# Another order of all steps, other conversion paths and more products of constants in an RWKV-7 and GELU kernel

## The chip, the cores and the metric

The kernel runs on one core of a Trainium2 chip. The metric is the device time of one execution in microseconds, the median of several runs. A core has five engines with a queue of instructions each: PE (matrix products, with a weight load PEld ahead of each), DVE (vector work), ACT (scalar functions and copies), POOL (general work), and SP, which here only issues DMA transfers. An engine takes its queue in order, and waits on semaphores where an instruction needs another engine's result.

## What is computed

Two blocks follow each other. The first is a recurrence over 768 time steps for 4 batches and 8 heads, with a 40 by 40 state for each; the second is a feed-forward block on the 3072 rows that come out.

```python
for t in range(S):
    y[:, :, t] = np.einsum('bhd,bhde->bhe', rt, state)
    Sa = np.einsum('bhde,bhe->bhd', state, at)
    state_decay = state * wt[:, :, None, :] - np.einsum('bhd,bhe->bhde', Sa, bt)
    state = state_decay + np.einsum('bhd,bhe->bhde', vt, kt)
...
h = x @ w_in                                   # (3072, 320) @ (320, 2048)
g = 0.5 * h * (1.0 + erf(h * inv_sqrt2))
return (g @ w_out).astype(np.float32)          # (3072, 2048) @ (2048, 320)
```

r, k, v, w, a and b are 32-bit floats. `w_in` and `w_out` come as 64-bit floats, 5.24 MB each, and the kernel makes 32-bit floats of them on the chip.

## The kernel before

Time is cut into 12 chunks of 64 steps. For each chunk all 32 batch-head pairs are worked on together. The products of the recurrence inside a chunk become small matrix products, and the dependence inside a chunk becomes the inverse of a triangular matrix per pair. The state passes from chunk to chunk. The output of each chunk, 256 rows, goes through the feed-forward block as soon as it is there.

**Order.** Every step is a small function, registered by its name, that issues the instructions of one piece of work. `order` (line 17) returns one long list of names with numbers, such as `nm.3` or `mh.0.2`, and the last two lines of the kernel perform them in that order. The scheduler is set to manual for all five engines, so each engine's queue is this list, restricted to the engine's own steps. The list also sets the use of four PSUM buffers (`bank0` to `bank3`): a step that calls `take` gets the buffer that has been given back longest, and waits for its last reader.

**Steps of a chunk c.**

- Loads, all on SP: `Lw La Lb Lk Lr LV` (line 433 and following, 320 KB each). From chunk 3 or 4 on some tensors are also loaded in a second layout (`Lwt Lbt Lkt Lv`).
- Decays: `lg` (log on ACT, L665), `cu` and `wT` (running sums of the logs as products with a mask, PE), `ec` and `ew` (exponentials, ACT, L722 and L708), `sb` and `sk` (scaled b and k, DVE or POOL).
- Transposes: `ta tb tk tr tv` on PE and `tm` on PE (L731); the copies out of PSUM are `sa sn kc rc vc tn`. From chunk 3 or 4 on most transposes run on DVE (L737).
- Products of pairs: `nm am vm` on PE, with masks applied by `nk ak vk` on DVE (L845).
- Inverse: for chunk 0 by squaring on PE, five rounds `qm.0` to `qm.4` with `qc qz qb qa` between them on ACT and DVE. For the others on POOL: `Ns` and `Nl` bring the blocks through DRAM into `Nb`, `ic` (L907 and L909) eliminates 31 columns with two instructions each, `Is`, `If` and `Ij` bring the result back into `Tt` and `T2`, and `tc_` on DVE, `jm`, `km` on PE and `jc kt0 kt1` join the blocks.
- State: `av` and `xm` (PE), `xc0 xc1` (copies), `sm` (PE), `sc` (DVE, L1108), `pk` and `pb` (PE), then `oa od om` (DVE) and `oc tm tn ym yc` make the next state and the output. `ox` moves parts of the output across partitions by DMA into `xt`.
- Feed-forward: `mh.c.p` for p from 0 to 7, 20 products each (L1231), reads `xt` and half of `w_in`'s converted form; `ge` is GELU (L1236). For chunks 0 to 2 the second product is `pm.c.n` (L1347, 16 products of 320 columns, four per chunk). From chunk 3 on it is seven products `m1` to `m7` of eight 160-column pieces each (L1270), with sums `s1` to `s4`, `e1` to `e6`. `so` writes the result.

**Conversion.** `w_in` is converted in units 0 to 9 of 512 columns, `w_out` in units 10 to 25 of 320 columns. They come by `Lf`, `Lf5` (units 0 to 9) and `Ls.f` (unit f + 10). For each unit `cp cm cs` (DVE) and `ce` (ACT) take the exponent, the mantissa and the sign. The mantissa's low part is then added and the result scaled by one of three paths:

- `cv`: two DVE instructions (L617, L618).
- `cl`, `cn` (ACT, L625, L632) and `cg`: two POOL instructions (L640, L641).
- `cl`, `cn` (ACT), `cx`: two PE products with the identity, and `cy`: one DVE product. No unit takes this path in the kernel before.

**Products of constants.** `warm_first` (six instructions) and `warm.4.i` (two instructions each) multiply constants into a PSUM buffer that nobody reads. There are 9 of the second kind before the change. The masks and constants themselves are set by POOL and DVE at the start (`identity`, `sums_mask`, `pads_...`, `warm_set`).

Of the kernel before, what the change touches and what calls it, by code (L numbers as in the profile page):

```python
# [16 lines left out]
def order(chunks, first_seven):  # L17
    return """
        of_half_set Lw.0 pads_a.0 sums_mask lg.0 cu.0 ec.0 Lb.0 sb.0 warm_set pads_w.0 pads_extra.2 pads_extra.0
        pads_extra.1 identity upper_mask pads_rows.0 pads_r.0 pads_VR.1 pads_r.1 first_ones.0 Tt_zero bias_set  # L20
# [4 lines left out]
        Lf.2.0.1 Lf.2.1.1 Lf5.1.1 Lk.1 warm.4.11 qa.1 qz.1 qb.1.0.v ce.0 cn.3 ce.3 ec.1 qb.1.1.a cs.0 cs.3 sb.1
        qm.2 qa.2 qz.2 qb.2.0.v warm.4.3 ta.1 warm.4.19 tb.1 iz.1 cg.3 sk.0.p sa.1 cp.5 cv.0 cm.5 cl.5 qc.2
        qb.2.1.a qm.3 qz.3 qb.3.0.v qa.3 tk.0 ce.5 sn.1 nm.1 kc.0 qb.3.1.a cn.5 nk.1 cs.5 cp.2 tr.0 cg.5 qm.4
        rc.0 ce.2 cl.4 qc.3 cl.7 tv.0 qa.4 cs.2 cp.7 cm.2 ce.7 cm.7 cn.7 ql cs.7 am.0 jm.0 ak.0 cv.2 cp.4 cm.4
# [1357 lines left out]
```

## Time and profile before

| | |
|---|---|
| median of 3 runs | 672.73 us (672.18 to 674.0) |
| the profiled execution | 673.18 us |
| its span, first to last instruction | 671.5 us |
| mean granted TensorE clock | 0.982 |
| POOL busy | 382.7 us (57%) |
| queue 1, all loads and stores | 73.78 MB, 60.2% of 16 DMA engines' span |

A profile page gives for each engine the time that it was busy, the span in 40 equal slices (a digit is the busy share in tenths), the clock that PE was granted, the share of the DMA engines, and groups of instructions by line. An L and a number name a line of the kernel. The timeline lists instructions by start and duration in us, with the number of them after an x, and in brackets how long the engine was idle before and what released it ("issue" where nothing that the profile shows did). Matmuls overlap, so a duration of a group reaches to the end of its last one.

### The profile page before, as it was taken

How to read it: one execution, taken by the hardware profiler on the slowest of the kernel's cores; microseconds unless marked ns; L12 is line 12 of the kernel's file. 1: busy time of each engine (PE TensorE's matmuls, PEld its weight loads, DVE VectorE, ACT ScalarE, POOL GpSimd, SP SyncE). 2: the span in 40 equal slices, each digit the busy share in tenths (PEclk: the TensorE clock that was granted, in tenths of full speed). 3: DMA queues.
4: the chain of work that ended last, by engine and by line, in shares of the span. 5: the costliest groups of instructions: out<-in, count | busy, mean ns of one | idle time of the engine just before them, and what ended most of it. 6: DMA issues, size and time to landing. Idle time of an engine off the chain costs nothing.

```text
span 671.5 us, 28177 instructions
## 1 busy us (share of the span) xinstructions
PE 643.9 (96%) x12480; PEld 560.8 (84%) x12480; DVE 421.5 (63%) x528; ACT 262.9 (39%) x329; POOL 382.7 (57%) x803
## 2 busy tenths in 40 slices
PE   4797889999999999999999999999999999999997
PEld 3576778888778878898898998997998988988987
DVE  1699988671664755885884777773885863723403
ACT  4456636522352452552623545242252344033040
POOL 4245873780585873871886860884872877830000
PEclk9796979999999999999999999999999999999999
DMA  9989488848867758647949757748658564130100
GB/s 153 159 169 163 98 189 170 152 91 137 151 112 138 137 109 148 138 86 136 155 85 163 141 115 136 124 86 155 130 108 141 109 121 84 38 60 3 26 16 21
DMA packets 302934, 78.10 MB, mean 116 GB/s; under 512 B 282556, under 2 KB 297692, under 8 KB 302812
## 3 DMA queue, kind: packets, MB, share of 16 engines
q1 hardware_dynamic: 301748, 73.78, 60.2%
q0 software_dynamic: 864, 2.36, 2.1%
q8 instruction: 98, 1.61, 1.0%
q14 instruction: 24, 0.20, 0.1%
q10 hardware_dynamic: 200, 0.16, 0.1%
HBM read 62.62 MB, written 9.70 MB: 108 GB/s over the span
## 4 chain that ended last, share of the span: by engine, by line
PE 80%; DVE 4%; SPq 2%; DMA 2%; issue 2%; POOL 1%; ACT 1%; DVEq 0%; POOLq 0%; ACTq 0%
PE bank L1231 28%; PE bank L196 22%; PE bank L1270 21%; PE bank L1347 8%; PE bank L731 2%; DMA v_pairs<-in_w_dram 1%; SPq L446 1%; POOL tmp L907 1%; DVE conv L609 1%; DMA T<-inv_blocks 1%; POOL W L909 1%; SPq L886 1%; DVE conv L588 0%; DVE kT L737 0%; DVE conv L602 0%
## 5 line engine op out<-in xcount | busy, mean ns | idle before, releaser
L1231 PE MATMUL bank<-xt,w_in_sb 64*128 64x256 f32 x1920 | 222.9, 384 | 0.1
L1231 PEld LDWEIGHTS bank<-xt,w_in_sb 64*128 64x128 f32 x1920 | 182.9, 188 | 25.2 <-issue 2.1
L907 POOL TENSOR_TENSOR tmp<-W,Nb 128x126 f32<-128x126 f32 (+22 forms) x341 | 151.7, 445 | 91.0 <-DMA Nb<-N_blocks 65.2
L909 POOL TENSOR_TENSOR W<-W,tmp 128x126 f32<-128x126 f32 (+22 forms) x341 | 160.4, 470 | 26.7
L1236 ACT ACTIVATE gt<-bank 128x1024 f32<-128x1024 f32 x48 | 48.9, 1023 | 104.5 <-PE bank L1231 104.4
L1270 PE MATMUL bank<-w_out_sb,gt 128*128 128x160 f32 x576 | 83.7, 301 | 0.0
L1270 PEld LDWEIGHTS bank<-w_out_sb,gt 128*128 128x128 f32 x576 | 79.2, 190 | 3.0 <-issue 2.0
L1347 PE MATMUL bank<-w_out_sb,gt 128*128 128x320 f32 x192 | 54.3, 437 | 0.7 <-issue 0.7
L1347 PEld LDWEIGHTS bank<-w_out_sb,gt 128*128 128x128 f32 x192 | 35.7, 190 | 15.6 <-issue 1.4
L1108 DVE TENSOR_TENSOR SM<-bank,upper 128x832 f32<-128x832 f32 x24 | 23.7, 1019 | 19.4 <-PE bank L196 19.3
L1007 DVE STREAM_TRANSPOSE conv<-Tt 128x512 f32<-128x512 f32 x11 | 7.8, 709 | 36.5 <-DMA Tt<-inv_blocks 36.4
L1056 DVE COPY Tt<-bank 32x512 f32<-32x512 f32 x9 | 6.2, 689 | 34.4 <-ACT Tt L1056 32.9
L898 POOL MEMSET W<- 128x512 f32 x11 | 5.8, 530 | 38.2 <-DMA inv_blocks<-W 38.2
L701 DVE TENSOR_TENSOR_SCAN kT<-spare,kT 128x256 f32<-128x256 f32 x32 | 24.1, 813 | 3.5 <-ACT kT L694 3.5
L1270 PE MATMUL bank<-extra,conv 128*128 128x160 f32 x176 | 25.7, 300 | 0.0
L1223 DVE TENSOR_TENSOR os<-os,bank 128x160 f32<-128x160 f32 x36 | 11.4, 318 | 22.6 <-PE bank L1270 12.1
L1158 DVE TENSOR_TENSOR st<-bank,st 128x832 f32<-128x832 f32 (+1 forms) x22 | 21.0, 981 | 6.4 <-PE bank L196 6.4
L1270 PEld LDWEIGHTS bank<-extra,conv 128*128 128x128 f32 x176 | 24.4, 190 | 0.2
L1223 DVE TENSOR_TENSOR conv<-gt 128x1024 f32<-128x1024 f32 x9 | 11.7, 1297 | 20.3 <-ACT gt L1236 20.3
L595 ACT ACTIVATE conv<-conv,rebias 128x320 uint32<-128x320 uint32 (+1 forms) x26 | 16.0, 622 | 21.2 <-DVE conv L588 21.2
L196 PEld LDWEIGHTS bank<-SM,Tt 64*64 64x64 f32 x768 | 17.5, 133 | 6.2 <-issue 3.4
L1236 ACT ACT_TABLE_LOAD x17 | 21.8, 1283 | 1.1 <-DVE N L845 0.8
(212 smaller groups left out, 1120.4 us busy)
## 6 DMA issues: line engine op xcount, KB each, us to landing
Nb<-N_blocks SPq DMA_DIRECT2D x22, 256.0 KB
b_rows<-in_b_dram SPq DMA_DIRECT2D x24, 160.0 KB
k_rows<-in_k_dram SPq DMA_DIRECT2D x24, 160.0 KB
VR<-in_v_dram SPq DMA_DIRECT2D x24, 160.0 KB
out_dram<-os SPq DMA_DIRECT2D x48, 80.0 KB
Tt<-inv_blocks SPq DMA_DIRECT2D x44, 64.0 KB
a_pairs<-in_a_dram SPq DMA_DIRECT2D x18, 144.0 KB
r_pairs<-in_r_dram SPq DMA_DIRECT2D x36, 72.0 KB
```

What stands on the lines that cost most here:

```text
L196: nc.tensor.matmul(o, lhsT, rhs, start=first, stop=True, skip_group_check=True)
L595: nc.scalar.activation(power, power, ACT.Relu, bias=rebias, scale=8.0)
L701: nc.vector.tensor_tensor_scan(logs[:, at:at + n], onward, logs[:, at:at + n], 0.0, ALU.mult, ALU.add)
L907: nc.gpsimd.tensor_tensor(t, W[:, :rows, j:j + 1].to_broadcast([P, rows, rest]), Nb[:, j:j + 1, j + 1:].to_broadcast([P, rows, rest]), ALU ...
L909: nc.gpsimd.tensor_tensor(W[:, :rows, j + 1:], W[:, :rows, j + 1:], t, ALU.add)
L1108: nc.vector.tensor_tensor(SM[:, g], pair_of(f"S{c}_", g).rearrange("p x i c -> p i x c"), pass_upper.unsqueeze(1).unsqueeze(1).to_broadcas ...
L1158: nc.vector.tensor_tensor(to, pair_of(f"QY{c}_", g)[:, :, :, cols], to, ALU.add)
L1223: nc.vector.tensor_tensor(to, one_, other, how)
L1231: nc.tensor.matmul(ph[:, x, s], w_in_sb[half(x), kt, p * P:(p + 1) * P], xt[half(x), kt], start=kt == 0, stop=kt == NK - 1)
L1236: nc.scalar.activation(gt[:, 4 * q:4 * q + 4].rearrange("p (x s) t -> p x s t", x=2), bank(f"ph{c}_{q}").rearrange("p x (s t) -> p x s t", ...
L1270: nc.tensor.matmul(po[:, n, :DM // 2], l_[:, f], r_[:, f], start=f == 0, stop=f == NF // 2 - 1)
L1347: nc.tensor.matmul(po[:, g, :DM], gt[:, f, g * P:(g + 1) * P], w_out_sb[:, f], start=f == 0, stop=f == NF - 1)
```

## The change

Only the list in `order` changes. All steps of the kernel before are performed, in another order on each of the five queues. These steps differ in kind:

- Units 3, 5, 9, 16 and 21 take the path `cv` instead of `cg`; units 1, 2 and 8 take `cg` instead of `cv`; unit 11 takes `cx` and `cy` instead of `cv`. So six units are on `cg` (eight before), nineteen on `cv` (eighteen before), one on `cx`.
- 21 steps `warm.4.i` stand in the list instead of 9, and `warm_first` stands at its head instead of behind `qm.1`.

In PE's queue five products of constants follow `warm_first`, ahead of `cu.0`; the others stand between the steps up to `tr.1`. In the kernel before the feed-forward products of chunk 0 are mixed with the preparation of chunks 1 and 2 (`mh.0.2 mh.0.3 av.1 ym.1 mh.0.0 tb.2 xm.1 nm.2 mh.0.1 tv.2 ...`); after the change they are `av.1 tr.2 ym.1 tb.2 xm.1 nm.2 mh.0.2 mh.0.3 mh.0.0 mh.0.4 mh.0.5 mh.0.1 mh.0.6 mh.0.7 tv.2 pm.0.0 pm.0.1 jm.1`.

The diff, up to `jm.1` and its end; the part left out is of the same kind:

```diff
--- before.py
+++ after.py
-        of_half_set Lw.0 pads_a.0 sums_mask lg.0 cu.0 ec.0 Lb.0 sb.0 warm_set pads_w.0 pads_extra.2 pads_extra.0
-        pads_extra.1 identity upper_mask pads_rows.0 pads_r.0 pads_VR.1 pads_r.1 first_ones.0 Tt_zero bias_set
-        pads_a.1 pads_w.1 first_ones.1 pads_VR.0 wT.0 warm.4.18 ew.0 tb.0 sn.0 La.0 Lf.0.1.0 ta.0 sa.0 nm.0 nk.0
-        qt Lw.1 Lf.3.1.0 lg.1 wT.1 ew.1 warm.4.26 qm.0 warm.4.16 cu.1 Lf.1.0.0 Lf.0.0.1 Lf.0.0.0 Lf.3.0.0 cl.3
-        Lf.1.1.0 Lf5.1.0 Lb.1 La.1 Lf.2.1.0 Lf.0.1.1 Lf5.0.1 Lk.0 qi.0.p pads_extra.3 qi.1.v cp.1 cp.0 qc.0 ce.1
-        qz.0 cm.1 qb.0.0.v qb.0.1.a qm.1 qc.1 cs.1 cv.1 cm.0 cm.3 cp.3 warm_first Lr.0 Lf.2.0.0 Lf5.0.0 LV.0
-        Lf.2.0.1 Lf.2.1.1 Lf5.1.1 Lk.1 warm.4.11 qa.1 qz.1 qb.1.0.v ce.0 cn.3 ce.3 ec.1 qb.1.1.a cs.0 cs.3 sb.1
-        qm.2 qa.2 qz.2 qb.2.0.v warm.4.3 ta.1 warm.4.19 tb.1 iz.1 cg.3 sk.0.p sa.1 cp.5 cv.0 cm.5 cl.5 qc.2
-        qb.2.1.a qm.3 qz.3 qb.3.0.v qa.3 tk.0 ce.5 sn.1 nm.1 kc.0 qb.3.1.a cn.5 nk.1 cs.5 cp.2 tr.0 cg.5 qm.4
-        rc.0 ce.2 cl.4 qc.3 cl.7 tv.0 qa.4 cs.2 cp.7 cm.2 ce.7 cm.7 cn.7 ql cs.7 am.0 jm.0 ak.0 cv.2 cp.4 cm.4
-        cg.7 qx vc.0 jc.0 Ls.2 Ns.1.1 Lf.1.0.1 Lf.1.1.1 warm.4.10 vm.0 Ns.1.0 Lw.2 Lf.3.1.1 Nl.1.0 Nl.1.1 Ls.0
-        Lf.3.0.1 Lr.1 LV.1 Ls.1 km.0 cp.9 vk.0 av.0 ce.4 cn.4 cs.4 cm.9 kt1.0 cg.4 ce.9 sk.1.v cl.9 cn.9 kt0.0
-        xc0.0 cs.9 xc1.0 cm.6 cp.6 ce.6 cs.6 sm.0 sc.0.1 sc.0.0 pk.0 pb.0 cv.6 cg.9 od.0.1 od.0.0 om.0.1 cp.8
-        om.0.0 lg.2 ce.8 cm.8 cs.8 cv.8 cp.10 cm.11 cp.11 wT.2 tk.1 tm.0 warm.4.29 kc.1 ew.2 ce.10 cu.2 tr.1 ec.2
-        ce.11 rc.1 cm.10 cs.10 cv.10 cs.11 cv.11 Ls.3 cm.12 cp.12 La.2 oc.0 tv.1 ta.2 warm.4.12 ox.0.1 ox.0.0
-        Ls.4 vc.1 tn.0 ce.12 cp.13 sa.2 am.1 vm.1 cs.12 cv.12 vk.1 cp.14 ce.13 ce.14 ak.1 Lb.2 Ls.9 Ls.5 cs.13
-        cm.13 cm.14 cv.13 cs.14 sb.2 cm.15 cp.15 cv.14 mh.0.2 mh.0.3 ge.0.1 av.1 ym.1 Ls.6 yc.1 ce.15 mh.0.0 tb.2
-        Ls.7 Lr.2 LV.2 sn.2 xm.1 nm.2 mh.0.1 cs.15 cm.16 cv.15 cp.16 cp.17 nk.2 cm.17 xc0.1 cn.16 ce.17 cl.16
-        ce.16 cs.17 cv.17 cp.19 ce.19 Ls.8 Ls.11 tv.2 vc.2 ge.0.0 xc1.1 cs.16 cm.19 cs.19 cv.19 cm.21 cp.21 Lk.2
-        Ls.10 Ls.13 Ns.2.1 ic.1.0.4 ic.1.4.8 ic.1.8.12 ic.1.12.16 ic.1.16.20 ic.1.20.24 ic.1.24.28 ic.1.28.31
-        Is.1.0.s Is.1.1.s cg.16 sk.2.v cp.18 Ns.2.0 Ls.15 Ls.12 If.1.1 Nl.2.1 If.1.0 Nl.2.0 Ij.1.1 Ij.1.0 cn.21
-        cl.21 ce.21 mh.0.4 mh.0.5 tr.2 cm.18 cs.21 ce.18 cs.18 cv.18 cg.21 cp.23 cm.20 cm.23 cp.20 tk.2 rc.2
-        ce.23 kc.2 cs.23 cv.23 cp.25 pm.0.0 mh.0.6 mh.0.7 cl.20 cn.20 ce.20 cs.20 cm.25 ce.25 cs.25 cv.25 tc_.1
-        unused.a unused.v cg.20 ge.0.2 jm.1 vm.2 iz.2 ic.2.0.4 ic.2.4.8 ic.2.8.12 ic.2.12.16 ic.2.16.20
-        pads_rows.1 ic.2.20.24 onward_set ic.2.24.28 ic.2.28.31 cp.22 ce.22 cs.22 cm.22 Ls.14 Lw.3 cv.22 cm.24
-        jc.1 km.1 vk.2 ge.0.3 kt1.1 La.3 Lr.3 pm.0.1 kt0.1 sm.1 cp.24 unused.r sc.1.1 sc.1.0 lg.3 cu.3 ec.3 ce.24
...
-        jc.11 ge.10.3 mh.10.2 km.11 mh.10.3 xc0.11 kt0.11 ge.10.1 kt1.11 sm.11 m1.10 m2.10 s1.10 sc.11.0 s2.10
-        sc.11.1 pk.11 pb.11 oa.11.1 s3.10 om.11.1 oa.11.0 om.11.0 e1.10 ox.11.1.a m4.10 m5.10 m6.10 ox.11.0 m3.10
-        e3.10 e2.10 s4.10 e4.10 m7.10 e5.10 e6.10 mh.11.6 mh.11.7 mh.11.0 mh.11.2 mh.11.3 mh.11.1 mh.11.4 mh.11.5
-        ge.11.3 ge.11.0 ge.11.1 m1.11 so.10.1 so.10.0 one_log ge.11.2 m2.11 s1.11 s2.11 s3.11 e1.11 e2.11 s4.11
-        m5.11 m3.11 m6.11 m7.11 e3.11 m4.11 e4.11 e5.11 e6.11 so.11.0 so.11.1
+        warm_set warm_first Lw.0 identity lg.0 pads_VR.1 first_ones.1 sums_mask pads_r.1 of_half_set pads_w.1
+        pads_w.0 pads_a.0 warm.4.0 warm.4.16 warm.4.10 warm.4.14 warm.4.15 pads_extra.0 pads_extra.1 pads_extra.2
+        first_ones.0 bias_set onward_set pads_rows.1 pads_r.0 iz.1 La.0 Lb.0 Lf.1.0.0 Lf.0.0.0 Lf.3.1.0 Lf.1.1.0
+        cu.0 wT.0 ta.0 warm.4.27 ec.0 ew.0 sb.0 tb.0 sn.0 sa.0 warm.4.28 nm.0 warm.4.21 warm.4.23 warm.4.3 Lw.1
+        Lf.0.1.0 Lf.2.0.0 Lf.0.1.1 Lf.2.1.0 Lk.0 Lf5.0.1 Lf.3.0.0 Lb.1 cm.1 upper_mask nk.0 qt qi.0.p pads_VR.0
+        qm.0 cp.1 qi.1.v qz.0 qb.0.0.v cp.0 lg.1 cn.1 ce.1 cs.1 cm.0 qc.0 qb.0.1.a ce.0 cl.1 cu.1 qm.1 warm.4.13
+        warm.4.11 warm.4.1 warm.4.26 cg.1 pads_a.1 sk.0.p cs.0 cv.0 qz.1 qa.1 ec.1 qb.1.1.a qc.1 cp.2 qb.1.0.v
+        cp.3 cm.2 sb.1 ce.2 ce.3 cn.2 cl.2 qm.2 wT.1 tb.1 warm.4.20 qz.2 cm.3 qb.2.0.v tk.0 qc.2 qb.2.1.a cs.3
+        qa.2 cv.3 cs.2 qm.3 qz.3 qb.3.0.v Lf.0.0.1 qa.3 pads_extra.3 cg.2 sn.1 kc.0 am.0 warm.4.22 La.1 Lf5.0.0
+        ta.1 Lf.1.0.1 LV.0 Lf.1.1.1 Lf.2.0.1 cp.4 qb.3.1.a ew.1 sa.1 cm.4 qm.4 qa.4 cl.4 qc.3 ce.4 nm.1 cm.5 cp.5
+        ak.0 cs.4 nk.1 Lr.0 Lf.3.0.1 Lf.3.1.1 Lf5.1.1 Lf.2.1.1 cn.4 ql LV.1 tv.0 vc.0 ce.5 cs.5 Ns.1.0 Lf5.1.0
+        tr.0 warm.4.4 jm.0 rc.0 vm.0 Lk.1 Ns.1.1 cg.4 Tt_zero qx cm.6 warm.4.29 warm.4.25 cv.5 cp.6 ce.6 cm.7
+        cn.7 cl.7 warm.4.18 cp.7 vk.0 jc.0 ce.7 cs.6 cv.6 cp.8 av.0 km.0 cs.7 Ls.1 Ls.0 Lr.1 Nl.1.0 Nl.1.1 tv.1
+        ce.8 kt0.0 cl.8 xc0.0 xc1.0 cs.8 kt1.0 cg.7 sm.0 cm.8 cn.8 vc.1 sk.1.v cp.9 sc.0.1 tk.1 ce.9 cl.11 kc.1
+        cm.9 sc.0.0 cs.9 cv.9 pk.0 pb.0 cg.8 cp.10 od.0.1 tr.1 warm.4.19 Lw.2 ic.1.0.4 ic.1.4.8 ic.1.8.12
+        ic.1.12.16 ic.1.16.20 ic.1.20.24 ic.1.24.28 ic.1.28.31 Ls.3 Lr.2 ce.10 rc.1 od.0.0 cm.11 cp.11 om.0.0
+        cs.10 cm.10 ce.11 cn.11 vm.1 lg.2 am.1 cx.11 La.2 Ls.2 Lb.2 cs.11 om.0.1 vk.1 ox.0.1 Ls.5 ak.1 cu.2 wT.2
+        tm.0 ec.2 oc.0 ew.2 cv.10 cy.11 cm.13 cp.13 cp.12 ta.2 sa.2 tn.0 ce.13 ce.12 cs.13 sb.2 cv.13 cs.12 cm.12
+        Ls.4 ox.0.0 av.1 tr.2 ym.1 rc.2 yc.1 cp.15 cv.12 Ls.6 tb.2 xm.1 sn.2 nm.2 ce.15 cm.15 cp.14 ce.14 xc0.1
+        cs.15 cv.15 cm.14 cs.14 cv.14 cp.16 nk.2 cm.16 mh.0.2 mh.0.3 ge.0.1 ce.16 cs.16 cv.16 mh.0.0 mh.0.4
+        mh.0.5 mh.0.1 mh.0.6 mh.0.7 Lk.2 Ls.11 Ls.7 Ls.8 cp.17 cm.17 ce.17 Ls.10 Ls.9 Lw.3 LV.2 Ns.2.1 cm.18
+        cp.18 ce.18 cs.17 cv.17 cs.18 cv.18 cp.19 cm.20 cm.19 cp.20 cl.20 ce.19 cn.20 ge.0.0 ce.20 xc1.1 tv.2
+        Ns.2.0 Ls.13 Ls.12 cs.19 cv.19 cp.21 ce.21 cm.21 cs.20 cs.21 cv.21 cp.23 Is.1.0.s Is.1.1.s Ls.15 Nl.2.0
+        Nl.2.1 If.1.0 Ij.1.0 If.1.1 Ij.1.1 Ls.14 La.3 Lr.3 Lb.3 Lv.3 cg.20 unused.v iz.2 unused.a ic.2.0.4
+        ic.2.4.8 ic.2.8.12 ic.2.12.16 ic.2.16.20 ic.2.20.24 ic.2.24.28 ic.2.28.31 pm.0.0 pm.0.1 cm.23 cp.22 ce.23
+        lg.3 cs.23 cv.23 cp.25 sk.2.v cm.25 ce.25 cs.25 cv.25 tc_.1 ce.22 vc.2 ge.0.2 cs.22 cm.22 cv.22 jm.1 vm.2
+        jc.1 vk.2 km.1 ge.0.3 kt1.1 kt0.1 cu.3 sm.1 ec.3 tk.2 sc.1.1 sc.1.0 cp.24 cm.24 kc.2 wT.3 pk.1 pb.1 ce.24
+        cs.24 cv.24 pm.0.3 oa.1.1 oa.1.0 om.1.1 om.1.0 Lk.3 am.2 od.1.1 pc.0.1 od.1.0 ta.3 ak.2 sb.3 sk.3.v
+        pm.0.2 LV.3 ox.1.1 Lw.4 tm.1 ew.3 oc.1 tn.1 pc.0.0 sa.3 av.2 tb.3 sn.3 ox.1.0 Lb.5 ym.2 yc.2 nm.3
...
+        ge.10.1 kt0.11 mh.10.4 mh.10.5 xc1.11 kt1.11 ge.10.2 sm.11 sc.11.0 s1.10 sc.11.1 pk.11 m1.10 pb.11
+        oa.11.0 s2.10 om.11.0 s4.10 oa.11.1 m2.10 om.11.1 ox.11.1.a s3.10 m5.10 m6.10 m4.10 m3.10 m7.10 e3.10
+        e1.10 e2.10 e4.10 e5.10 e6.10 ox.11.0 mh.11.6 mh.11.7 mh.11.2 mh.11.4 mh.11.0 mh.11.3 mh.11.1 mh.11.5
+        ge.11.3 ge.11.0 ge.11.1 so.10.0 m1.11 so.10.1 ge.11.2 m2.11 s1.11 s2.11 s3.11 s4.11 m5.11 m6.11 m3.11
+        m7.11 m4.11 e1.11 e2.11 e4.11 e3.11 e5.11 e6.11 so.11.0 so.11.1
```

## The prediction

> **What bounds the kernel now.** I read three parts of the page first: busy time, the forty slices, the chain that ended last.
>
> ```profile
> PE 643.9 (96%) x12480; PEld 560.8 (84%) x12480; DVE 421.5 (63%) x528; ACT 262.9 (39%) x329; POOL 382.7 (57%) x803
> ...
> PE   4797889999999999999999999999999999999997
> ...
> PEclk9796979999999999999999999999999999999999
> DMA  9989488848867758647949757748658564130100
> ```
>
> PE is full from the seventh slice on (a slice is 16.8 us). What is lost lies in the first six, where the granted clock dips too and the DMA engines are near full for four. The table of stretches, in columns stretch, PE, PEld, DVE, ACT, POOL (busy us and instructions), PEclk, DMA share, GB/s, places it:
>
> ```profile
> 20.00:23.40 3.40, 0.32 (x6) 0.14 (x5) 3.32 (x4) 0.78 (x2) 3.27 (x4) 1.00 1.28 141
> 23.40:30.20 6.80, 5.82 (x129) 3.63 (x129) 3.84 (x8) 1.93 (x3) 0.60 (x3) 0.50 0.89 160
> ...
> 50.70:54.10 3.40, 2.17 (x114) 1.86 (x110) 3.40 (x7) 3.38 (x7) 1.17 (x1) 1.00 0.98 199
> 54.10:64.30 10.20, 9.49 (x212) 7.42 (x212) 8.66 (x12) 7.50 (x12) 6.01 (x5) 0.50 0.96 165
> ...
> 70.00:88.20 18.20, 17.16 (x364) 14.52 (x366) 17.70 (x30) 10.05 (x14) 15.70 (x33) 1.00 0.45 94
> 88.20:91.60 3.40, 1.48 (x44) 1.05 (x44) 3.40 (x6) 1.93 (x3) 2.85 (x8) 1.00 0.82 233
> 91.60:98.50 6.90, 6.90 (x122) 6.09 (x116) 6.80 (x15) 2.42 (x3) 5.88 (x14) 0.51 0.83 171
> 98.50:122.20 23.70, 23.70 (x308) 19.40 (x304) 18.47 (x38) 14.05 (x23) 9.54 (x20) 1.00 0.93 182
> 122.20:300.00 177.80, 176.24 (x3631) 146.76 (x3630) 110.64 (x121) 73.11 (x83) 117.48 (x265) 1.00 0.68 125
> ```
>
> Three times PE is partly idle for 3.4 us and then runs 7 to 10 us at half clock. DVE is busy 17.7 of 18.2 us from 70 to 88: there its queue paces the work. After 122 PE hardly rests. So the time is: when PE becomes full, plus the PE work still queued then. The timeline gives the points that I use:
>
> ```profile
> 18.94 1.13 PE L196 MATMUL bank<-cum_m,ident 128*128 128x512 f32 x2
> 24.38 1.92 PE L196 MATMUL bank<-N,st 32*32 32x32 f32 x123 [3.43 <-issue]
> 26.23 2.08 PE L196 MATMUL bank<-cum_m,ident 128*128 128x512 f32 x2
> ...
> 84.28 4.59 PE L1231 MATMUL bank<-xt,w_in_sb 64*128 64x256 f32 x40
> 90.80 2.30 PE L196 MATMUL bank<-VR,late 64*64 64x104 f32 x64 [1.92 <-DVE late L845]
> ...
> 122.19 0.75 PE L196 MATMUL bank<-conv,spare 32*32 32x32 f32 x64
> ```
>
> A product of constants takes 1.1 us at full clock (18.94) and 2.1 at half (26.23). `mh.0.2` starts at 84.28, `av.1` waits 1.92 us at 88.9, `jm.1` starts at 122.19.
>
> **The sum.** It is made against the profiled execution: 673.18, span 671.5, so 1.7 around it; the median is 0.45 lower.
>
> Behind `jm.1`: add up PE's queue after it by the durations in the rows (`mh` 2.26, `pm` 4.35, second-level products 2.17, the 64-instruction groups 0.7 to 1.5). The old queue holds 540.7 us, and the span has 549.3 left; 8.6 is tail (4.2), small waits, rounding. The new one holds 537.3: `pm.0.1` now stands ahead of `jm.1` (4.35 less) and `tk.2` behind it (0.95 more). So 545.9 follow `jm.1`.
>
> When `jm.1` starts in the new order, in four steps.
>
> (1) Start. Three first products and five of constants, 16 instructions of 512 columns, stand ahead of `cu.0`. Before, the first matmul ran at 7.66 and the durations halved at about 13.1, 5.5 us later. The new first one can start at 1.4; with the same 5.5 us some six instructions run at 0.85 and ten at 0.43, to 11.1. `cu.0` and `wT.0` (1.24 and 1.1 at full clock) end at 13.5, against 12.05; the following transposes are faster, and `nk.0` ends near 19.8 against 19.4. Cost 0.4; bounds: -1, or +3 if the clock rises at 13.1 anyway.
>
> (2) Inverse of chunk 0. Before, PE stopped 3.43 us inside `qm.0`, released by nothing but "issue". The page's 98 instruction packets of queue 8 carry 1.61 MB, 16.4 KB each, for 24960 PE instructions: 255 a packet, and the first starts at 21.5. So this stop is code coming late over full DMA engines. The new order has nearly as many instructions ahead of that point, so I keep the stop. By the Trainium skill, "Runtime: NRT & Kernel Launch", section "Instruction fetch mechanics", crossing such a block of 256 instructions is mostly hidden; by that the lead below would be 5 us, not 2.5; this stop speaks against it. Without the stop the sum gives 662 to 663, still in the forecast. What goes is `warm.4.16`, 1.9 us between `qm.0` and `cu.1`: `qm.1` starts near 28.1 (30.3 before), `qm.2` near 33.6 (36.1). Lead 2.5. Four products then stand in each such wait of some 3.5 us and end with it. Before, the half clock from 54.1 to 64.3 stretched `jm.0` to `av.0` by about 4.7; whether three products there prevent it I take as even. So `sc.0.0`, which ended at 70.7, ends at S = 66 to 68; I take 67. Bounds: 63.5 and 73.
>
> The rule that speaks against these twelve added products: "TensorE: Matmul & The Clock Gate", Part 1 of the Trainium skill, has the clock fall after one idle window of about 3.4 us, so that shorter waits need no filling. The rows disagree: 2.17 busy of 3.4 us (50.7) and 1.48 (88.2) were each followed by half clock. By the rule the twelve would only cost queue time, up to 10.8 us at 0.9.
>
> (3) From S to `mh.0.2`. DVE's queue paces: `cs.9 cv.9 cp.10`, two `od`, `cm.11 cp.11 om.0.0` take 5.1 us by their rows (0.7, 1.37, 0.49, 0.9, 0.98, 0.68), then `cs.10 cm.10 cs.11 om.0.1` to S+7.5, `vk.1` 8.7, `ak.1` 9.9, `cv.10 cy.11` 11.5. The PSUM buffers hand this pace to PE: counting their rotation, `cx.11` waits for `om.0.0`, `cu.2` for `om.0.1`, `wT.2` for `vk.1`, `tm.0` for `ak.1`, `av.1` for `cy.11`. Behind each stands all of PE; the waits sum to about 1 us, because `pb.0 tr.1 vm.1 am.1` fill the beginning. Then `tr.2 ym.1 tb.2 xm.1 nm.2`, and `mh.0.2` at S+19.8. Before it was S+13.6, but `av.1` to `nm.2`, 7.5 us, were still to come, and 4.9 more went in the 1.92 wait and the half clock. A second bound is SP: `ox.0.1` stands behind 12.6 MB of loads; at the 160 GB/s of the first four slices that is 76 to 78. Then 4.2 us for it, 2 for two `Ls`, 4 for `ox.0.0` (75.09 to 83.3 in the rows), 2 to land: 88. I take 88.
>
> (4) Eight `mh` 18.1, `tv.2` 2.1, `pm.0.0` and `pm.0.1` 8.7: `jm.1` at 116.9. Its other input comes over SP: `Is.1` follows nine loads and `Ns.2`; thirteen loads took 22.5 us between 83.4 and 105.9, 1.73 each, so it is issued at 107 as before, and `tc_.1` can follow at about 116. I add 1 us: 118.
>
> 118 + 545.9 + 1.7 = 665.6, less 0.45: **665**.
>
> **Costs taken as nothing.** Conversions: units 16 and 21 go from POOL to DVE (+2 x 1.16), unit 11 to PE and one DVE product (-1.16 + 0.35, a new form bounded by 0.3 and 0.7 from the nearest PSUM reads; 0.9 on PE, in the count of step 3). DVE gets 1.5 us, POOL loses 3.7, ACT about 1. DVE's sum up to `tc_.1` is 96.5 against 94.5, under 29 us of `mh` and `pm`. POOL's `ic.1` starts near 66, when `Nb` has landed (0.9 MB more ahead of it, 5.7 us), as it did at 66.6 after `cg.9`; without the cover, each us late is one at `jm.1` after 9 us of slack. In later chunks every load and every `nm` to `jm` (60 us) has similar distances in both orders; the thin ones, `km.1` to `sm.1` (1.2 us for two 0.59 copies) and `ym` to `xm` in chunks 1 and 2, cost 0.5 together.
>
> **Rivals.**
> A, no lead in front: the first products run at half clock, or the added ones only take queue time and the stops recur. S = 70.7 to 73 gives `jm.1` at 120.4 to 122.7, 667.5 to 669.8. For it: code packets still come late. Against: three dips had idle time that now is filled.
> B, slower: SP holds the blocks of T. Nine loads, `Ns.2` and two more stand between `ox.0.0` and `Is.1`. Two `VR` loads took 2.92 us at 64.1; at 2.9 each nine take 26 instead of 15.6, `jm.1` comes at 127.5, PE idles 10 us and pays 3.4 more at half clock: 678. It decides from 2.9 us a load on. For it: DMA near 0.9 in that stretch. Against: 1.73 measured.
> C, nothing in the end: the lead is given back in waits of half a us at each of eleven chunk changes: 671 to 674.7.
>
> **How the numbers follow.** Forecast 0.52 (660 to 667), A 0.16, B 0.22 (675 to 682), C 0.10. The range 657 to 677 takes in S from 63.5 and half of B. About 0.3% (2 us) is what a measurement here can tell: faster 0.68, same 0.10, slower 0.22.
>
> **What would show it.** Step 1: `cu.0` at 11 to 12, at full clock. Step 2: an idle PE near 22 again, `qm.2` before 35, `sc.0.0` ended by 68. Step 3: no half clock around 90, `mh.0.2` at 86 to 89 directly after `nm.2`. Step 4: `pm.0.1` ahead of `jm.1` without a gap, `jm.1` at 117 to 119; after it as full a PE row as now. Wrong if `cu.0` comes after 14, if PE stands still ahead of `jm.1`, or if the PE row shows gaps after 120.

## The result and the profile after

The changed kernel takes 682.46 us (median of 4 runs, 681.91 to 683.21), the kernel before 673.37 beside it (4 runs, 672.18 to 674.2): ratio 1.0137, 95% interval 1.0117 to 1.0158. It is 9.1 us slower, 17 above the forecast and 5 above the range. The profiled execution took 683.21, its span 681.5.

The page, with the same rows as before:

```profile
PE 656.8 (96%) x12508; PEld 566.4 (83%) x12508; DVE 415.2 (61%) x531; ACT 265.6 (39%) x329; POOL 376.8 (55%) x799
...
PE   9798899999999999999999999999999999999997
...
PEclk9999979999999999999999999999999998999999
```

The clock row has lost two of its three dips and has a small one near 565 us (0.89 from 560 to 575). The loss is hardly to be seen in these rows: PE's digits are 9 from the sixth slice to the last but one, and a wait of 1 us in a slice of 17 doesn't change a digit. The table of stretches (columns as in the prediction) shows the front:

```profile
50.70:54.10 3.40, 2.34 (x117) 1.89 (x120) 3.37 (x6) 2.46 (x5) 2.00 (x2) 1.00 0.95 152
54.10:64.30 10.20, 9.17 (x243) 6.80 (x236) 10.07 (x16) 8.07 (x14) 3.00 (x2) 1.00 0.64 140
...
78.90:82.40 3.50, 1.56 (x29) 1.32 (x32) 0.00 (x0) 1.62 (x3) 2.92 (x8) 1.00 1.21 175
82.40:92.60 10.20, 9.55 (x176) 8.45 (x170) 8.14 (x13) 4.06 (x5) 8.82 (x18) 0.50 0.37 99
...
122.90:300.00 177.10, 173.85 (x3556) 144.66 (x3557) 110.43 (x123) 68.74 (x78) 117.36 (x258) 1.00 0.66 123
```

There is no half clock up to 82, then one from 82.4 to 92.6, behind a stretch in which PE was busy for 1.56 of 3.5 us and DVE not at all. From 122.9 to 300 PE rests for 3.25 us, against 1.56 before. The points of the timeline that the prediction used (PE, and one row of DVE):

```profile
11.36 1.24 PE L197 MATMUL bank<-w_tile,cum_m 128*128 128x320 f32 x4
21.41 1.29 PE L197 MATMUL bank<-N,st 32*32 32x32 f32 x128
26.16 1.05 PE L197 MATMUL bank<-turned,st 64*64 64x64 f32 x29 [2.19 <-ACT st L986]
...
80.94 1.06 PE L732 MATMUL bank<-ident,a_pairs 128*128 128x128 f32 x8 [1.94 <-DMA a_pairs<-in_a_dram]
...
94.27 2.00 PE L1232 MATMUL bank<-xt,w_in_sb 64*128 64x256 f32 x16
...
122.90 0.74 PE L197 MATMUL bank<-conv,spare 32*32 32x32 f32 x64 [0.39 <-DVE conv L1008]
```

```profile
83.46 0.60 DVE L589 TENSOR_SCALAR conv<-w_out_sb 128x320 uint32<-128x320 uint32 x1 [5.74 <-DMA w_out_sb<-in_moe_w_out_dram]
```

`cu.0` starts at 11.36, `qm.0` runs without a stop, `mh.0.2` starts at 94.27 and `jm.1` at 122.90. The last two views are PE's waits behind `jm.1`, the kernel before first, the changed one second: releaser, sum in us, times, longest.

```profile
PE bank L196 <- issue: 0.9, 1, 0.9
PE bank L196 <- DVE conv L1007: 0.7, 1, 0.7
PE bank L1347 <- issue: 0.7, 1, 0.7
PE bank L196 <- DMA T<-inv_blocks: 0.5, 1, 0.5
```

```profile
PE bank L197 <- issue: 2.0, 2, 1.2
PE bank L197 <- DVE conv L1008: 1.8, 2, 1.4
PE bank L197 <- DMA T<-inv_blocks: 1.6, 3, 0.7
PE bank L1232 <- issue: 1.5, 1, 1.5
PE bank L197 <- DVE SM L1109: 0.9, 2, 0.8
PE bank L197 <- DVE VR L846: 0.7, 1, 0.7
```

Four waits of 2.8 us in all became thirteen of 9.1 (two for ACT, 0.6 in all, are left out here), none above 1.5 us, with seven releasers. `conv L1007` and `L1008` are `tc_`, so these rows and those of `T` mean the blocks of T.

To see what the waits cost, I took each PE step's time up to the next step, less the median that this kind of step takes in the two traces, and call the rest **excess**: waits, half clock, stretched steps. Behind `jm.1` the steps' medians sum to 542.5 us before and 539.0 after (3.5 less, as forecast). The excess is 2.6 before and 15.4 after. With `jm.1` 0.7 later: 0.7 + 12.8 - 3.5 = 10.0, the difference of the two profiled times.

### The profile page after: what moved, and what is told of

The parts are those of the page before. It is cut to its first block, busy times and chain, and to the rows that moved or that the text cites. A ratio compares the mean times of both kernels' runs of the same rounds, so it can differ in the third digit from the quotient of the medians.

```text
span 681.5 us, 28225 instructions
## 1 busy us (share of the span) xinstructions
PE 656.8 (96%) x12508; PEld 566.4 (83%) x12508; DVE 415.2 (61%) x531; ACT 265.6 (39%) x329; POOL 376.8 (55%) x799
## 4 chain that ended last, share of the span: by engine, by line
PE 59%; SPq 14%; DMA 8%; POOL 8%; DVE 5%; issue 4%; ACT 1%; DVEq 0%; POOLq 0%; ACTq 0%
PE bank L1232 20%; PE bank L1271 18%; PE bank L197 17%; POOL tmp L908 4%; POOL W L910 4%; PE bank L1348 3%; SPq L434 2%; SPq L533 2%; DMA inv_blocks<-W 2%; SPq L887 2%; DMA Nb<-N_blocks 1%; SPq L922 1%; DMA T<-inv_blocks 1%; PE bank L732 1%; DMA Tt<-inv_blocks 1%
## 5 line engine op out<-in xcount | busy, mean ns | idle before, releaser
L910 POOL TENSOR_TENSOR W<-W,tmp 128x126 f32<-128x126 f32 (+22 forms) x341 | 158.4, 465 | 26.7
L1008 DVE STREAM_TRANSPOSE conv<-Tt 128x512 f32<-128x512 f32 x11 | 7.8, 711 | 38.0 <-DMA Tt<-inv_blocks 38.0
L1159 DVE TENSOR_TENSOR st<-bank,st 128x832 f32<-128x832 f32 (+1 forms) x22 | 21.2, 988 | 10.5 <-PE bank L197 10.5
L899 POOL MEMSET W<- 128x512 f32 x11 | 5.8, 529 | 33.8 <-DMA inv_blocks<-W 33.8
L702 DVE TENSOR_TENSOR_SCAN kT<-spare,kT 128x256 f32<-128x256 f32 x32 | 22.6, 763 | 1.6 <-ACT kT L695 1.6
L197 PE MATMUL bank<-SM,Tt 64*64 64x104 f32 x768 | 20.6, 252 | 1.1 <-ACT SM L1090 0.8
```

Of the source, the lines that this page charges most:

```text
L197: nc.tensor.matmul(o, lhsT, rhs, start=first, stop=True, skip_group_check=True)
L702: nc.vector.tensor_tensor_scan(logs[:, at:at + n], onward, logs[:, at:at + n], 0.0, ALU.mult, ALU.add)
L910: nc.gpsimd.tensor_tensor(W[:, :rows, j + 1:], W[:, :rows, j + 1:], t, ALU.add)
L1159: nc.vector.tensor_tensor(to, pair_of(f"QY{c}_", g)[:, :, :, cols], to, ALU.add)
```

## The experiments

Theory at first: SP issues in order, and the changed order puts loads ahead of T's blocks and of what the front waits for. Rivals: the front alone or the rest alone carries it; waits that go return elsewhere, because transfers and code are late wherever the DMA engines are full. The runs came from four chips, on which single runs of the kernel before ranged from 670 to 685 us, so intervals are wide and each ratio is to the kernel before on the same chip. A trace is one execution, and not always a middle one: that of h1 is 3.5 us above its median, that of e_main_blocks 6.5, that of b_repeat 3.6, so differences of a few us between two traces are weak evidence. The table gives for each: runs, median, ratio with interval, and from its trace the start of `jm.1`, the excess from `jm.1` to `jm.5` and behind `jm.5`.

| label | runs, median us | ratio (interval) | jm.1 | excess to jm.5, behind |
|---|---|---|---|---|
| before, first trace | 4, 673.37 | 1 | 122.2 | 0.7, 1.8 |
| b_repeat | 10, 674.13 | 1.0004 (0.9967 to 1.004) | 119.1 | 4.9, 5.2 |
| after, first trace | 4, 682.46 | 1.0137 (1.0117 to 1.0158) | 122.9 | 4.9, 10.5 |
| a_repeat | 6, 682.68 | 1.0123 (1.0059 to 1.0186) | 121.3 | 4.9, 10.7 |
| h1_new_front_old_rest | 5, 683.97 | 1.0100 (1.0031 to 1.017) | 125.3 | 9.3, 8.0 |
| h2_old_front_new_rest | 4, 684.20 | 1.0118 (1.0054 to 1.0182) | 118.5 | 5.7, 13.1 |
| e_front_loads | 10, 683.04 | 1.0109 (1.0074 to 1.0143) | 122.7 | 3.8, 9.8 |
| e_main_blocks | 10, 681.42 | 1.0081 (1.004 to 1.0122) | 123.9 | 8.9, 10.1 |
| e_both | 12, 680.80 | 1.0089 (1.0054 to 1.0124) | 121.3 | 4.9, 7.8 |
| a_nine | 12, 681.26 | 1.0093 (1.0056 to 1.013) | 122.9 | 2.3, 12.0 |
| b_late | 12, 680.03 | 1.0066 (1.0028 to 1.0103) | 120.2 | 2.8, 8.9 |
| e_first | 5, 706.30 | 1.0467 (1.0421 to 1.0514) | 124.1 | 4.4, 33.8 |
| e_first_front | 6, 709.02 | 1.0520 (1.0459 to 1.0581) | 121.0 | 5.7, 31.9 |
| b_first | 6, 703.38 | 1.0410 (1.0357 to 1.0463) | 118.3 | 6.3, 33.2 |
| t_new | 6, 732.01 | 1.0862 (1.0807 to 1.0916) | 123.8 | 66.2 in all |
| t_old | 6, 710.45 | 1.0551 (1.0494 to 1.0608) | 118.2 | 42.6 in all |
| t2_new | 6, 683.92 | 1.0125 (1.0086 to 1.0165) | 121.8 | 5.5, 10.2 |
| t2_old | 12, 679.10 | 1.0080 (1.0046 to 1.0114) | 118.2 | 5.3, 6.9 |
| l_new | 12, 676.26 | 1.0037 (1.0003 to 1.0072) | 122.6 | 1.5, 6.8 |
| l_old | 12, 671.57 | 0.9959 (0.9924 to 0.9994) | 118.7 | 3.0, 1.4 |

**Front or rest.** Both lists joined, up to and from `xm.2`.

```diff
 h1: up to xm.2 the list of after.py, behind it that of before.py
 h2: up to xm.2 the list of before.py, behind it that of after.py
```

> All steps up to xm.2 in the new order, the rest in the old one. Counted by durations, jm.1 starts 0.7 us later than in the kernel before but 3.4 us less PE work follows it; the waits of PE after jm.1 sum to 2.6 us in the kernel before and 15.4 after the change. If the loss lies in the rest of the order: about 670 us, some 3 us faster than before. If the front carries the loss onward (later inputs, another phase of the queues): 679 to 682.

> The mirror image: old order up to xm.2, the new one after it. If the loss lies in the rest: 122.2 + 542.5 of work + 15.4 of waits + 4.2 of tail = 684 span, 686 us, the slowest of all. If the front carries the loss: 672 to 675.

Both are as slow as the changed kernel, so either half of the new order is enough for the loss, and the two don't add. h2 says something clear: with the old front `jm.1` comes at 118.5, and the new rest still loses 18.8 behind it. h1 says less: the old rest behind a foreign front has 17.3, though behind its own it had 2.6 and 10.1. That a rest is fitted to its front is how I read it; no run shows it by itself.

**Single loads and blocks on SP.**

```diff
 e_front_loads (after.py; e_both has both)
-Ls.3 Lr.2 La.2 Ls.2 Lb.2        DVE: cp.12 ta.2 sa.2
+Ls.3 La.2 Ls.2 Lb.2 Lr.2        DVE: sa.2 cp.12
 e_main_blocks
-If.2.1 La.4 Ij.2.0 Ij.2.1 ... Lb.7 If.7.1 Nl.8.0 Nl.8.1 Lbt.9 Ij.7.0 Ij.7.1
+If.2.1 Ij.2.0 Ij.2.1 La.4 ... If.7.1 Nl.8.0 Nl.8.1 Ij.7.0 Ij.7.1 Lb.7 Lbt.9
-Ns.10.0 If.9.1 If.9.0 Ns.10.1 Lk.10 Ij.9.1 Nl.10.1 Ij.9.0 Nl.10.0
+Ns.10.0 Ns.10.1 If.9.1 If.9.0 Ij.9.1 Nl.10.1 Ij.9.0 Nl.10.0 Lk.10
 b_late (before.py): Lbt.4 ahead of Ij.2.1, Lbt.9 ahead of Ij.7.0, Ns.10.0 ahead of If.9.1, Lk.10 ahead of Ij.9.1
```

> The changed kernel with Lr.2 issued behind Lb.2 instead of ahead of La.2, and cp.12 behind sa.2 on DVE. Theory: in the changed kernel PE waited 1.9 us for La.2 at 79 and DVE 5.7 us for Ls.2 at 78, and half clock from 82 to 92 followed; La.2 and Ls.2 now are issued 2.7 us earlier. mh.0.2 then starts near 89 instead of 94.3 at full clock, and the time falls by 4 to 5 us, to 678. Rival: the loads only change places at a DMA rate that is the limit, tr.2 waits for Lr.2 instead, and the time stays within 1 us of the changed kernel.

> The changed kernel with the transfers of the inverse's blocks ahead of loads on SP at three places: Ij.2 ahead of La.4; Ij.7 ahead of Lb.7 and Lbt.9; Ns.10.1 beside Ns.10.0 and Lk.10 behind Nl.10. Theory: PE waited for these blocks 1.1 us in chunk 2, 1.0 in chunk 7 and 3.2 in chunk 10 (with the half clock that followed): 5 us less, 677. Rival: the waits in the rest are code that comes late and copies that are tight, and the time stays at 682; or other transfers become the late ones.

> The changed kernel unchanged, beside the next three on one chip. If its loss lies in its order, the ratio is again 1.012 to 1.016 and the profiled run has PE waits for T's blocks near 167, 426, 519 and 565 us. If its loss was chance in one set of runs, the ratio is under 1.008 and the waits stand elsewhere.

> The changed kernel with both sets of moves at once: in front Lr.2 behind Lb.2 and cp.12 behind sa.2; later the blocks of T for chunks 2 and 7 ahead of a load, Ns.10.1 right behind Ns.10.0 and Lk.10 behind Nl.10. Theory SP (the loss is SP's order, blocks behind loads): 7.4 us of waits named in the profile go (5.8 later, 1.9 in front), ratio 1.001 to 1.004 to the kernel before. Rival (waits that go return behind the next engine): ratio 1.008 or more, and the PE waits after jm.1 sum to 11 us or more.

> The kernel before with only the SP order around three groups of blocks made like the changed kernel's: Lbt.4 ahead of Ij.2, Lbt.9 ahead of Ij.7.0, Ns.10.0 ahead of If.9 and Lk.10 ahead of Ij.9. Nothing else moves. Theory SP: jm.2, km.7 and jm.10 had 0.2, 1.1 and 1.1 us of slack and get 2, 2 and 5 us later blocks, so PE waits 5 to 7 us more, ratio 1.006 to 1.011. Rival: ratio 0.998 to 1.003, the blocks had slack in this order.

e_front_loads moved the waits and did not remove them, as its rival said: `tr.2` then waited 2.39 us for `Lr.2`, DVE 4.21 us for another load of `w_out`, half clock came again (granted clock 0.66 from 80 to 100 us), and `mh.0.2` started at 92.14, not near 89. e_main_blocks got 681.42 where its theory said 677. The unchanged kernel repeated its ratio; of the four places that I had named, its trace waits again at two, `km.2` (1.3 us) and around `mh.9.5` and `km.10`, and no longer near 426 and 519. `b_late` came out as the theory said: three groups of late blocks cost the old order 0.66%, 4.4 us (interval 0.28 to 1.03%). But the repairs gave little: e_both 0.9% against 1.2%, its interval overlaps. The repaired waits at `km.2`, `km.7`, `km.9` and `mh.9.2` are gone in its trace, and `mh.5.4` (2.7 us), `km.6` and `pm.1.1` (0.8 and 0.9) have come. That is what the rival said (a ratio of 1.008 or more; 12.7 us of excess behind `jm.1`, where it had 11 or more). That the repair removed the four waits is not shown: in a_repeat's trace, where nothing was repaired, three of them are under 0.2 us too, and only that at `km.2` is there.

**The products of constants.**

```diff
-warm.4.0 warm.4.14 warm.4.15 warm.4.27 warm.4.28 warm.4.21 warm.4.23 warm.4.13 warm.4.1 warm.4.20 warm.4.22 warm.4.4 warm.4.25
```

> The changed kernel without the 13 products of constants that the kernel before does not have (26 PE instructions of 512 columns, read by nobody). If they hold the clock in front, half clock comes back ahead of 60 us, sc.0.0 ends at 70 or later, and the time is 1 to 4 us longer than the changed kernel's. If they only stand in PE's queue, sc.0.0 ends at 67 or earlier and the time is the same or up to 1 us shorter; jm.1 waits for tc_.1 and can't gain more.

Without 13 of the 21 the granted clock from 20 to 60 us falls from 0.91 and 1.00 (a_repeat) to 0.78 and 0.83, here in columns as above, a_nine:

```profile
20.00:40.00 20.00, 15.13 (x274) 12.22 (x266) 16.45 (x25) 11.60 (x18) 8.84 (x9) 0.78 0.97 171
40.00:60.00 20.00, 17.59 (x464) 14.09 (x462) 17.20 (x26) 13.27 (x21) 4.80 (x4) 0.83 0.83 133
```

In the eleven traces with the new front and all 21 the clock is 0.91 to 1.00 in both stretches, so the products hold it there. They don't always hold it through `jm.0` to `av.0`: from 54 to 64 us it is 1.00 in seven of the eleven and 0.83 to 0.89 in four, against 0.72 in a_nine. `pb.0` comes at 68.8 in a_nine, and at 66.4 to 68.3 in the eleven; `jm.1` at 122.9, inside their 121.0 to 125.3. The time isn't longer: 0.93% against 1.23%. No gain of theirs can be seen at the end.

**All loads out of the way of T.** From the end of each inverse (chunks 2 to 10) to the last block, every load and store goes behind the block.

```diff
 chunk 7 of e_first, SP's queue; the other chunks in the same way
-Lk.8 so.5.1 La.9 Lwt.9 If.7.0 Ns.8.1 Ns.8.0 Lb.7 If.7.1 Nl.8.0 Nl.8.1 Lbt.9 Ij.7.0 Ij.7.1
+If.7.0 Ns.8.1 Ns.8.0 If.7.1 Nl.8.0 Nl.8.1 Ij.7.0 Ij.7.1 Lk.8 so.5.1 La.9 Lwt.9 Lb.7 Lbt.9
```

> The changed kernel with every load and store that SP issued between the end of an inverse (chunks 2 to 10) and the last block of its T moved right behind that block, 21 in all, and the five vector steps that read them behind tc_ of the chunk. Theory SP (what the changed order loses after jm.1 is loads ahead of T's blocks): in chunks 6, 7 and 9 the time from the end of ic to tc_ falls from 12.5 to 15, 25 and 14.5 us to 10 to 12, excess PE time after jm.1 falls from 15.5 us to 6 or less, ratio 1.000 to 1.004. Rival (the waits return behind other steps): ratio 1.008 or more.

> The same, with Lr.2 behind Lb.2 and cp.12 behind sa.2 in front besides. Theory SP: 1 to 2 us less than the one before, ratio 0.997 to 1.002. Rival: as the one before.

> The kernel before with the same rule: 14 loads and stores that SP issued between the end of an inverse and the last block of its T moved behind that block, and two vector steps. Theory SP: its waits after jm.1 summed to 2.6 us in the profiled run, so 0 to 2 us less, ratio 0.997 to 1.000; if its slow runs too are late blocks, the spread of its runs shrinks. Rival (loads that come later are late themselves): ratio 1.003 or more.

> The kernel before unchanged, for a profile on this chip beside the others. Ratio 0.997 to 1.003. Theory SP: its excess PE time after jm.1 is 2 to 6 us, and any wait over 1 us is at km or behind tc_.

All three are 28 to 34 us slower than the kernel before. PE's waits in e_first:

```profile
PE bank L195 <- ACT Js L1030: 15.8, 1, 15.8
PE bank L195 <- DVE conv L736: 7.0, 1, 7.0
```

ACT's timeline there gives the chain:

```profile
438.56 1.28 ACT L693 ACT_TABLE_LOAD   x1 [20.09 <-DVE kT L736]
439.86 1.06 ACT L693 ACTIVATE kT<-kT 128x1024 f32<-128x1024 f32 x1
...
441.56 0.38 ACT L1030 COPY Js<-bank 128x256 f32<-128x256 f32 x1
```

`lt.9` (L693) stands ahead of `jc.7` (L1030) on ACT and reads what `tw.9` makes of `Lwt.9`. I had moved the load and `tw.9` and not `lt.9`, so the load held the very chain that it was moved away from. In b_first ACT waits 17.2 us at an `lt` in the same way. In chunks 2, 3 and 6 `tc_` did come 1.3 to 2.4 us sooner after its inverse than in a_repeat, in chunk 4 it came 4.4 us later, and the excess up to `jm.5` hardly fell (4.4 against 4.9). Of the three chunks that the theory named, 6 came down to the forecast 10 to 12 us (about 11), 7 and 9 did not (about 21 and 14). So these three runs say little of T. b_repeat's trace has 10.1 of excess, where the first trace of the same kernel had 2.6.

**T never late.** In t_new and t_old `If` and `Ij` of chunks 3 to 11 stand ahead of the first `ox` of the chunk before; t2 takes the dependence away with them: each chunk's T is then read from the block that chunk 1 wrote, and what the later inverses store is left unread.

```diff
 t2_new and t2_old, besides the order of t_new and t_old
-        rows = inv_blocks[c % 2].rearrange("j z n (s q) t -> q (j z n) s t", q=2)
+        rows = inv_blocks[int(c == 1)].rearrange("j z n (s q) t -> q (j z n) s t", q=2)
-        inv = inv_blocks[c % 2]
+        inv = inv_blocks[1]
-                            in_=inv_blocks[c % 2][j, 1].rearrange("(n z) s t -> z s n t", z=2)[1])
+                            in_=inv_blocks[1][j, 1].rearrange("(n z) s t -> z s n t", z=2)[1])
```

> The changed kernel with the loads of T's blocks (If, Ij) of chunks 3 to 11 issued ahead of the first ox of the chunk before, so that they read the blocks of an older chunk: the recurrence's result is wrong from chunk 3 on, the amount of work and of DMA is the same, and T is never late. Theory T (late T is what the changed order pays for): 3 to 8 us less than the changed kernel, 675 to 679 where that is 682.5, and no wait for T after chunk 3. Rival DMA (transfers and code packets come late wherever the DMA engines are full, T only happens to be one of them): within 2.5 us of the changed kernel, other waits grow. Rival queue (the order itself): the same.

> The kernel before with the same edit, the same part wrong. Theory T: 1 to 4 us less than the kernel before, so that the distance of the pair falls from 9 us to 5 or less. Rivals: within 2.5 us of it, the distance stays at 8 to 10.

> The changed kernel where every chunk's T is read from a block tile that only chunk 1 writes (the results of the inverses of chunks 2 to 11 are stored, and not read), with If and Ij of chunks 3 to 11 ahead of the first ox of the chunk before: the output is wrong from chunk 2 on, work and DMA bytes stay, SP never waits for an inverse there and T is never late. Theory T (half of the loss after jm.1 is late T): 4 to 8 us less than the changed kernel, ratio 1.001 to 1.006, no PE wait for T after 170 us, excess after jm.1 under 10 us. Rival DMA (with T out of the way other transfers and code packets are late as often): ratio 1.010 or more.

> The kernel before with the same edit, the same part wrong. Theory T: 1 to 4 us less, ratio 0.994 to 0.999, so that the distance of the pair is 3 to 6 us. Rival DMA: ratio 0.999 to 1.003, the distance stays at 8 to 10.

t_new and t_old missed their aim. In several chunks `Is` stands ahead of the moved `If` in the list, so `If` read its own chunk's blocks and SP waited for the inverse, 51 us in t_new, with `ox` behind it; PE waited 42.6 us for `xt` behind 122 us. They show only what a wait on SP costs. t2 did its work; PE's waits in t2_new behind 122 us:

```profile
PE bank L1229 <- DMA xt<-xt: 3.9, 2, 2.7
PE bank L1229 <- issue: 3.1, 3, 1.6
PE bank L194 <- DVE SM L1106: 1.8, 2, 1.6
...
PE bank L194 <- DVE conv L1005: 1.2, 1, 1.2
```

One wait for T is left, 1.2 us. In its place stand `xt`, which now comes behind the blocks (3.9 us), and code. The ratio is 1.0125, as without the edit, so theory T's forecast for this kernel (1.001 to 1.006) fails. But the edit has a price of its own: it makes the old order 0.80% slower (0.46 to 1.14), some 5 us, where the theory had 1 to 4 us less. The distance of the pair falls to 4.8 us, inside the 3 to 6 that the theory had for it, though by the old order's loss and not by the new one's gain. If the new order pays the same price, it has won about as much from T never being late. So **the run does not settle what late T costs**: taking it away in this way gains nothing, and a way without the price was not tried.

**Fewer bytes.**

```diff
 l_new, l_old: without La Lb Lk Lr LV Lbt Lkt Lv of chunks 6 to 11 (48 loads; the tiles keep older chunks' data)
```

> The changed kernel without 48 loads: of chunks 6 to 11 only Lw and Lwt are loaded, the other eight tensors' tiles keep older chunks' data, so the output is wrong from there; all engines' work stays. Rival DMA: PE's waits after 310 us go, 6 to 10 us less than the changed kernel, 673 to 677. Theory T: about the same, since the blocks of T then land early. Rival queue: within 2.5 us.

> The kernel before with the same 48 loads left out. Rival DMA and theory T: 2 to 5 us less, and the pair's distance falls to 5 us or less. Rival queue: the distance stays at 8 to 10.

The DMA engines' share from 310 to 600 us falls from 0.62 to 0.31. l_new is at 1.0037 and a_repeat at 1.0123, so 5.8 us go; of the kernel before 3.0 go (1.0004 to 0.9959). The pair's distance falls from 9 us to 4.7 or, by the ratios, 5.3. So late transfers make a part of the loss, and about half of the distance remains without these loads; by the spread of the twelve runs of each, an estimate, 3 to 7 us of it. What is left behind `jm.5` in l_new, 6.8 against 1.4 in l_old, begins with this row:

```profile
315.81 0.48 PE L1227 MATMUL bank<-xt,w_in_sb 64*128 64x256 f32 x2 [2.22 <-issue]
```

The stop at `mh.4.1` is in every trace that has the changed order's 12508 matmuls in their places (1.9 to 3.3 us of excess; 0.8 to 1.2 in t_new, e_first and e_first_front), but neither in a_nine nor in h2, which have 26 and 28 fewer ahead of it. In h2 a stop of 0.5 us stands at the next step, `sm.5`, at the same number in PE's queue, about the 6080th matmul. The packets of queue 8, which bring instructions, show what it is: in `after` one of 16 KB ends at 317.60 and PE goes on at 319.11, in l_new one ends at 314.34 and PE goes on at 315.81. So it is code that comes late at a fixed place of the queue. The loads left out did not halve the traffic ahead of it (DMA share 0.77 in `after` and 0.56 in l_new over the 16 us before `mh.4.1`), so l_new doesn't show whether fewer loads would remove it.

Nor is code the difference of the pair. The old order has stops of the same kind, at `am.3` and `pm.1.0` (0.7 to 1.5 us of wait at `pm.1.0` in all seven of its traces). Counting stops of 0.4 us or more behind `jm.1`, code makes 3.5 and 3.6 us in the two traces of the changed kernel, 1.6 and 2.7 in those of the kernel before, and 2.2 in l_new against 3.2 in l_old.

## Why the prediction was wrong

The sum was 118 + 545.9 + 1.7 - 0.45. Measured in the profiled execution: 122.9 + 558.6 + 1.7. So 4.9 us are missing up to `jm.1` and 12.7 in "Behind `jm.1`".

- **Step 1, the start: right.** `cu.0` at 11.36, at full clock; 11.1 was forecast.
- **Step 2, the inverse of chunk 0: right end, wrong way.** The code stop in `qm.0` that I kept did not come, and `qm.1` began at 26.2 instead of 28.1. Then it waited 2.19 us for ACT and `qm.2` 1.79 for DVE: `qm.2` at 33.66 (33.6 forecast), `sc.0.0` ended at 67.2 (67). No half clock from 54 to 64 in this execution; in four of the other ten traces with this front and these products there was some. `pk.0`, which follows, started at 65.85, and in the other seven traces of the old front at 64.8 to 66.7: against those the lead is gone. By the Trainium skill, "Runtime: NRT & Kernel Launch", section "Instruction fetch mechanics", crossing a block of code is mostly hidden. At `qm.0` the trace now agrees; at `mh.4.1` it doesn't (1.5 us of issue, 2.2 in l_new), nor does the old front, which stops in `qm.0` in all eight of its traces (1.5 to 3.4 us).
- **Step 3, from S to `mh.0.2`: failed by 6.3 us** (88 forecast, 94.27). Two chains came late together. The bound by SP was too short: `ox.0.1` was issued at 79.7 (78 at the latest by my working) and took 7.0 us instead of 4.2, then `Ls` 2.2, `ox.0.0` 3.3 and 2 to land. And DVE, which I had pacing the work, stood still for 5.74 us at `cp.12`, because its load `Ls.2` stands behind `Lr.2` and `La.2` on SP: I hadn't put `Ls.2` and `La.2` on SP's clock. `Ls.2` then took from 76.57 to about 83.4 to land. PE waited 1.94 and 0.65 us and got half clock behind it, so that `nm.2` ended at 94.2 too. The rule of "TensorE: Matmul & The Clock Gate", Part 1 of the Trainium skill, that one idle window of 3.4 us makes the clock fall, is again too mild: PE was busy 1.56 of 3.5 us. Moving the two (e_front_loads) only moved the waits. In no trace of the new front does `mh.0.2` start before 91.1, and in eight of the eleven PE waits there 0.5 to 3.6 us for `xt`: the 88 was too early in every execution, by 3 us at least.
- **Step 4: failed by 4.9 us.** PE, 6.3 us late from step 3, ended `pm.0.1` at 122.5, and that is where the lateness comes from. `Is.1` was issued at 110.7, not at 107, behind eleven loads and `Ns.2`, and `tc_.1` ended at 122.8. That is rival B's mechanism at 3.7 us instead of 10, but PE waited only 0.39 us for it. The lead that the sum counted on was wrong at its other end too: in the executions whose front is the old one `jm.1` comes at 118.2 to 120.2 (seven traces), and 122.2 was one late execution. In those with the new front it comes at 121.0 to 125.3. The dips themselves are no chance: all eight traces of the old front have half clock in places (0.83 to 0.91 from 20 to 40 us). But the start of `jm.1` that I measured the gain against was 2 to 4 us later than in the other seven, and I had booked 4.2 as lead.
- **"Costs taken as nothing": failed, the largest term.** I had written "In later chunks every load and every `nm` to `jm` (60 us) has similar distances in both orders", and 0.5 us for the thin ones. The excess behind `jm.1` is 15.4, in five executions of the new rest 13.6 to 18.8, against 2.6 and 10.1 for the old order behind its own front. Behind `jm.5` alone it is 9.8 to 13.1 against 1.8 and 5.2. So the step that failed is the assumption that an order with similar distances has similar waits; the sum has 0.5 us for what measured 12.7. How tight it already was: in the first trace of before, `jm.2` starts 0.2 us after its `tc_`, `jm.8` 0.1, and six others 0.8 to 1.4. In the changed kernel's trace five `jm` start within 1.4 us of their `tc_`, where the kernel before has these eight, so a count of such places does not say which order waits more.
- **The rivals.** C (given back at each chunk change, half a microsecond at each of eleven: 671 to 674.7) had the right kind and place; it had a chance of a tenth, and its 6 to 10 us are half of the 17 measured.

The account in medians: `jm.1` some 4 us later with 3.5 us more work done by then, so the front comes out even; the 9 us are made behind it. Shown: where the loss lies; that late blocks cost the old order 4.4 us if it is given them (b_late); that with half the bytes of the later chunks gone 5.8 us of the new order's time go, and 3.0 of the old one's (l_new, l_old). Not shown: what late T costs the new order, since the edit that takes it away (t2) has a price of its own. Open: which property of the order makes the 5 us that stay between l_new and l_old; code it is not, by the stops counted above, and for the rest I have no experiment. No kernel that I tried with the reference's whole work beats the kernel before.

## What to carry to other kernels

In a hand-ordered kernel whose bound engine is 96% busy, a new order is not worth what its changed stage is worth: put a term for new waits in the later stages into the sum, and don't take it as nothing because the distances look alike (here it was 12.7 us of 671.5). Take a second trace of the unchanged kernel where you can, before you book its dips as gains: here the start of `jm.1` differed by 3 us and the excess behind it by 7.5 between two executions of one kernel. When you move a load, move all that stands in order behind its readers, on every engine, or leave it.

## What the runs showed of the hardware

- Half clock followed stretches in which PE was busy for 1.48 to 2.17 of 3.4 us, and once more 1.56 of 3.5; the 50.7 to 54.1 stretch of the changed kernel, at 2.34 of 3.4, was followed by full clock.
- In the twenty traces PE stopped 66 times for 0.4 us or more with nothing but "issue" to release it. Each of these stops ended 1.3 to 1.8 us after a 16 KB packet of the instruction queue had ended; a matmul taken at random lies so in one case of ten.
- The places of these stops are numbers in PE's queue, not steps: the matmul that waits has 221 ahead of it in all eight traces of the old front, 3401 in all seven of the old order, and 6079 to 6084 in eleven traces, in `mh.4.1` of the new order, in `sm.5` of h2 and in `am.6` of t2_old. Not every execution stops at each of them.
